# Attention in steps of four heads instead of two, its matmuls grouped by the way they divide TensorE's array

## The chip, the cores and the metric

The kernel runs on one core of a Trainium2 chip. The metric is the time of one execution on the device in microseconds (us). The engines have short names in the profile: PE is TensorE's matmuls, PEld its weight loads, DVE is VectorE, ACT is ScalarE, POOL is GpSimd, and SP issues most of the DMAs. Each engine works through its own instructions in the order in which the program lists them.

## What is computed

Attention over 2 batches of 8 heads with 768 positions and head dimension 64, then a mixture of 8 experts of which each token takes two, then an MLP, all in float32:

```python
scores = q @ k.T / 8 - slope[h] * dist          # kept: the first 8 keys, and the 96 last before the query
a = softmax(where(keep, scores, -1e9))
x = (a @ v) as [1536 tokens, 512]
logits = x @ w_gate + log1p(exp(x @ w_noise)) * noise     # top two experts, softmax over them
y = sum over the two experts of weight * (relu(x @ w1[e]) @ w2[e])
out = silu(y @ w_in) @ w_out
```

## The kernel before

The 1536 queries are 12 tiles of 128 (six of a batch). A tile's queries see at most 232 keys: the 96 before the tile, the 8 global ones and its own 128 (`WK`); the first tile of a batch (0 and 6) sees only its own 128 (`wd`). All of it is written in one order by hand (`tc.manual_schedule()`), so an engine takes its instructions in the order in which the loop at the end of the attention part calls the helpers.

That loop runs over steps `s`, four for a tile `n`, each with one pair of heads `c`. A step does, in this order: `scores(s)` (two matmuls that each use 64 rows of the array, one for each head of the pair, into the banks `h` and `y0` or `y1`; VectorE then adds the bias and takes the minimum, one head at a time, into `sb` and `mn`); `expo(s)` (ScalarE's exponential of each head into `pn`, with its sum); `p_t(s - 2)` (TensorE transposes the `pn` of two steps ago through the identity, ScalarE copies the result to `pts`); and `av(s - 3)` (the products with the values, each of which uses 64 columns of the array, into the bank `y3`; after a tile's last pair VectorE copies them to `xt`). A float32 matmul that is no transpose runs as two passes, which the trace lists one by one.

Between these the loop puts, by the step's place in its tile: the loads of q, k and v two tiles ahead; `prep_q` and `prep_k` for the next tile (four transposes each, copied by ScalarE and VectorE to `qh` and `kth`); `post` of the tile before, as a generator in parts (the gates' products `pg` with 64 columns each, the transposes of `xt`, VectorE's scaled copy `xn`, the gates' transpose, and VectorE's product `lp` and sum into `L`); the load and the split of the experts' first weights; and `route`, a generator in thirteen pieces, once for each group of tiles (0 to 3, 4 to 7, 8 and 9 inside the loop). Its pieces are small VectorE operations on logits; piece 8 is the maxima and the selection, piece 10 the matmuls that count with the selection (L620 to L623), piece 12 ends in the scatters of the tokens' rows by POOL. `routed(k)` takes the next k pieces; `R1` and `R2` say how many come before and after the step's transposes.

Transposed results go through three banks in turn (`tbank`: two of `tp` and `y2`): a transpose waits until the copy out of its bank, three uses earlier, is done.

After the loop come the experts and the MLP, which the change leaves as they are.

Of the kernel before, what the change touches and what calls it, by code (L numbers as in the profile page):

```python
# [20 lines left out]
P = 128  # L21
# [229 lines left out]
def attn_moe_mlp(ctx, tc, q, k, v, n_global, n_local, w_gate, w_noise, noise,  # L251
# [95 lines left out]
    # how many tokens chose an expert, and whether one chose more than two  # L347
# [10 lines left out]
    # three banks in turn  # L358
# [10 lines left out]
    # the values of a query tile's keys: the last PV of the tile before, the batch's first  # L369
    # NG (the global ones), those of its own tile, two neighbours in a partition  # L370
# [40 lines left out]
    # the tensor engine's clock rises only after it has been busy for a while  # L411
# [17 lines left out]
    # dist where a key is kept, far above any distance where not: a key of its own tile that comes  # L429
    # after the query counts as further off than any local one  # L430
# [23 lines left out]
    def late_consts():  # L454
# [9 lines left out]
        # summed over the partitions, this is the expert's first slot  # L464
# [36 lines left out]
    def scores(s):  # L501
# [4 lines left out]
        ps = [bank("h", 2), bank(f"y{s % 2}")]  # L506
        for j in range(2):
            r = slice(j * D, (j + 1) * D)
            nc.tensor.matmul(ps[j][:, :wd], QH[n][r, c, :], kt[r, c, o:o + wd], start=True, stop=True)  # L509
        SB[s] = awk.tile([P, 2, WK], F32, name="sb", bufs=3)  # L510
        MN[s] = awk.tile([P, 2], F32, name="mn", bufs=3)
        bt = bias1 if i else bias0
        for j in range(2):
            nc.vector.tensor_tensor_reduce(SB[s][:, j, :wd], ps[j][:, :wd], bt[:, 2 * c + j, :], 1.0, 3.0e38,  # L514
                                           op0=OP.add, op1=OP.min, accum_out=MN[s][:, j:j + 1])

    def expo(s):
        n, c = divmod(s, HP)
        wd = WK if tiles[n][1] else P
        if c == 0:  # L520
            SM[n] = xnp.tile([P, H], F32, name="sm", bufs=3)
        PN[s] = awk.tile([P, 2, WK], F32, name="pn", bufs=3)
        for j in range(2):
            nc.scalar.activation(PN[s][:, j, :wd], SB[s][:, j, :wd], AF.Exp, bias=MN[s][:, j:j + 1], scale=-1.0,  # L524
                                 accum_out=SM[n][:, 2 * c + j:2 * c + j + 1])

    def p_t(s):
        n, c = divmod(s, HP)
        nb, kr = (2, WK // 2) if tiles[n][1] else (1, P)
        p = tbank().rearrange("p (j a t) -> p j a t", j=2, a=2)  # L530
        for j in range(2):
            for a in range(nb):
                nc.tensor.transpose(p[:kr, j, a, :], PN[s][:, j, a:nb * kr:nb], ident)  # L533
        PT[s] = awk.tile([P, 2, 2, P], F32, name="pts")
        nc.scalar.copy(PT[s][:kr, :, :nb], p[:kr, :, :nb])

    def av(s):
        n, c = divmod(s, HP)
        i = tiles[n][1]
        if c == 0:  # L540
            OT[n] = bank("y3").rearrange("p (c t) -> p c t", c=HP)
        nb, kr = (2, WK // 2) if i else (1, P)
        for a in range(nb):
            for j in range(2):
                nc.tensor.matmul(OT[n][j * D:(j + 1) * D, c, :], VT[n][:kr, 2 * c + j, a, :], PT[s][:kr, j, a, :],  # L545
                                 start=(a == 0), stop=(a == nb - 1))
        if c == HP - 1:
            XT[n] = xnp.tile([P, HP, P], F32, name="xt", bufs=2)
            nc.vector.tensor_copy(XT[n], OT[n])

    # the gates' products of a token for each of the heads, whose sums are yet to be divided by
    def post(n, psum, direct=False):
# [3 lines left out]
        pg = psum()[:, :P]  # L556
        if direct:
            for c in range(HP):
# [3 lines left out]
        else:  # L562
            for u in range(2):
                for j in range(2):
                    nc.tensor.matmul(pg[j * D:(j + 1) * D], wgn[:, 2 * j + u, :], XT[n][:, 2 * j + u, :],
                                     start=(u == 0), stop=(u == 1))
# [3 lines left out]
        yield  # L570
# [6 lines left out]
        if direct:  # L577
            logits(pg)
        else:
            g = xnp.tile([P, P], F32, name="pg", bufs=2)  # L580
            nc.vector.tensor_copy(g, pg)
# [4 lines left out]
        if not direct:  # L586
            pl = psum()[:, :P]
            nc.tensor.transpose(pl, g, ident)
            yield
            logits(pl)  # L590

# [4 lines left out]
    # an expert's rows in blocks; of the first one's, the first two are read early  # L596
# [59 lines left out]
    # the slots of the other experts that no token took: all of them, if a token chose more than two  # L656
    # experts, as a slot in between is left out then
# [32 lines left out]
    routing, later = [], []  # L690
    R1, R2 = (0,1,1,1), (1,2,0,2)
    NS = NT * HP

    def start(g):
        if next(g, g) is not g:
            later.append(g)
# [10 lines left out]

    prep(0)
# [3 lines left out]
    for s in range(NS + 3):  # L712
        n, c = divmod(s, HP)
        if s < NS:
            scores(s)
            expo(s)
        if s == 0:
            prep(HP // 2)
# [6 lines left out]
        if c == 0:  # L725
            later = [g for g in later if next(g, g) is not g]
        routed(R2[c])
        if n < NT:
            if c == 0 and 2 <= n + 2 < NT:
                load_qk(n + 2)  # L730
                load_v(n + 2)
            if c == 1 and n + 1 < NT:
                start(prep_q(n + 1))
            if c == 2 and n + 1 < NT:
                start(prep_k(n + 1))
            if s == 1:
                late_consts()
            if s == 2:
                load_small()
            if s == 6:  # L740
                zero_fill()
        if c == 3 and n >= 1:
            start(post(n - 1, tbank))
        if c == 0 and n >= 2 and n - 2 in groups:
            routing.append(route(*groups[n - 2], tbank, True))
        if c == 1 and 2 <= n <= 10:
            load_half(n - 2)
        if c == 3 and 2 <= n <= 7:
            split_high(n - 2, True)
            split_low(n - 2, True)  # L750
    for g in later + routing:
        for _ in g:
            pass
    actx.close()

# [447 lines left out]
```

## Time and profile before

| | |
|---|---|
| time, median of 3 runs | 763.61 us (763.43 to 772.5) |
| span of the profiled execution | 765.0 us |
| TensorE busy | 744.1 us, 97% of the span |
| VectorE, ScalarE, GpSimd busy | 450.1, 270.8, 192.8 us |
| attention, to the first matmul of the experts | the first 137.55 us of the span |

The page gives the profiled execution by its span, from the first to the last instruction; the times of the runs are those of other executions. Busy time of TensorE is partly modelled, since matmuls are pipelined, so the starts of its instructions say more than their lengths. A bracket behind a row of a timeline says how long the engine was idle before it and what ended that.

### The profile page before, as it was taken

Reading aid. Unit: us, or ns where it says so; the run is one execution under the profiler, and the core shown is the slowest. Engines: PE = TensorE matmul, PEld = TensorE weight load, DVE = VectorE, ACT = ScalarE, POOL = GpSimd, SP = SyncE. Lnnn points to the kernel's source line nnn. Section 1 sums busy time; section 2 is a strip of 40 time slices with the busy share of each in tenths; the row PEclk is TensorE's granted clock in tenths of the full one; section 3 lists DMA queues with packets and bytes.
Section 4 is the critical chain, followed back from the end, with each engine's and each line's share of the span. In section 5 each row is a group of like instructions: output and inputs, shape, how many; then the busy total and the mean of one; then the engine's idle time right before and its main releaser. Section 6 shows DMA issues by size and latency. Waiting matters only on the chain.

```text
span 765.0 us, 11233 instructions
## 1 busy us (share of the span) xinstructions
PE 744.1 (97%) x4087; PEld 586.9 (77%) x4087; DVE 450.1 (59%) x986; ACT 270.8 (35%) x635; POOL 192.8 (25%) x178
## 2 busy tenths in 40 slices
PE   8998898999999999999999999999999999999996
PEld 4665565788777777777787777888888888888895
DVE  5567484647888898887888765574233332322332
ACT  6665573334333434434333345352122111111111
POOL 4135412334533234243434120422012000000000
PEclk9999896999999999999999999999999999999998
DMA  9868554267868587786868554652002010000100
GB/s 163 203 145 235 144 153 167 84 204 232 284 213 284 144 293 223 247 236 222 244 210 277 181 163 139 202 198 84 28 27 56 15 55 1 1 0 1 56 1 32
DMA packets 96278, 111.78 MB, mean 146 GB/s; under 512 B 36479, under 2 KB 65727, under 8 KB 96216
## 3 DMA queue, kind: packets, MB, share of 16 engines
q1 hardware_dynamic: 89096, 94.50, 41.7%
q0 software_dynamic: 6608, 16.10, 6.3%
q8 instruction: 34, 0.56, 0.3%
q10 hardware_dynamic: 512, 0.40, 0.2%
q14 instruction: 28, 0.23, 0.1%
HBM read 84.00 MB, written 32.51 MB: 152 GB/s over the span
## 4 chain that ended last, share of the span: by engine, by line
PE 87%; DVE 5%; issue 3%; ACT 2%; DMA 1%; another core or an unknown queue 1%; POOL 0%; SPq 0%; POOLq 0%; ACTq 0%; DVEq 0%
PE h L785 13%; PE h L788 12%; PE h L786 12%; PE y L820 11%; PE y L816 11%; PE y L821 11%; PE y L805 4%; PE y L545 3%; PE h L509 3%; PE tp L767 2%; PE tp L533 2%; ACT pn L524 1%; PE y L533 1%; PE tp L569 1%; PE tp L494 1%
## 5 line engine op out<-in xcount | busy, mean ns | idle before, releaser
L785 PE MATMUL h<-xh,u1h 128*128 128x448 f32 (+3 forms) x544 | 184.9, 352 | 0.0
L786 PE MATMUL h<-xh,u1l 128*128 128x448 f32 (+3 forms) x544 | 179.3, 341 | 0.0
L820 PE MATMUL y<-u2h,hh 128*128 128x512 f32 x368 | 145.3, 395 | 0.6 <-ACT hh L795 0.6
L821 PE MATMUL y<-u2l,hh 128*128 128x512 f32 x368 | 144.5, 393 | 0.0
L1112 DVE CAST hh<-h 128x256 fp32r<-128x256 f32 (+1 forms) x64 | 35.7, 558 | 149.8 <-ACT h L1111 149.7
L785 PEld LDWEIGHTS h<-xh,u1h 128*128 128x128 f32 x544 | 102.5, 188 | 26.0 <-issue 15.4
L788 PE MATMUL h<-xl,u1h 128*128 128x448 f32 (+3 forms) x544 | 120.0, 342 | 0.0
L786 PEld LDWEIGHTS h<-xh,u1l 128*128 128x128 f32 x544 | 102.7, 189 | 9.7
L816 PE MATMUL y<-u2h,hl 128*128 128x512 f32 x368 | 108.7, 394 | 0.7 <-DVE hl L796 0.7
L788 PEld LDWEIGHTS h<-xl,u1h 128*128 128x128 f32 x544 | 92.3, 189 | 9.0
L1111 ACT ACTIVATE h<-h 128x256 f32<-128x256 f32 (+1 forms) x64 | 30.4, 475 | 183.1 <-PE h L788 182.1
L887 POOL TENSOR_TENSOR co<-ct,co 128x512 f32<-128x512 f32 x32 | 41.4, 1292 | 175.5 <-issue 141.9
L816 PEld LDWEIGHTS y<-u2h,hl 128*128 128x128 f32 x368 | 68.9, 188 | 17.8 <-DVE hl L796 2.1
L820 PEld LDWEIGHTS y<-u2h,hh 128*128 128x128 f32 x368 | 69.2, 188 | 13.7 <-ACT hh L795 1.0
L821 PEld LDWEIGHTS y<-u2l,hh 128*128 128x128 f32 x368 | 69.2, 188 | 12.1
L1054 ACT ACTIVATE hw<-h 128x64 f32<-128x64 f32 x64 | 14.4, 224 | 130.6 <-DVE hl L796 125.2
L524 ACT ACTIVATE pn<-sb,mn 128x232 f32<-128x232 f32 (+1 forms) x96 | 44.8, 467 | 39.4 <-DVE mn L514 38.6
L770 DVE TENSOR_TENSOR xl<-tp,xh 128x512 fp32r<-128x512 f32 (+1 forms) x44 | 28.1, 643 | 45.6 <-ACT xh L769 45.5
L795 ACT ACTIVATE hh<-h 128x384 fp32r<-128x384 f32 (+2 forms) x72 | 31.3, 435 | 47.7 <-PE h L788 44.4
L796 DVE SCALAR_TENSOR_TENSOR hl<-h,hh 128x384 fp32r<-128x384 f32 (+2 forms) x72 | 34.4, 478 | 20.4 <-ACT hh L795 19.3
L324 POOL TENSOR_TENSOR u1l<-ra,u1h 128x1024 fp32r<-128x1024 f32 x16 | 41.9, 2617 | 5.6 <-ACT u1h L319 5.4
L514 DVE CUSTOM_DVE_ANT_0 sb<-h,bias 128x232 f32<-128x232 f32 (+1 forms) x48 | 18.2, 379 | 39.6 <-PE y L509 23.1
(219 smaller groups left out, 1053.8 us busy)
## 6 DMA issues: line engine op xcount, KB each, us to landing
ra<-in_moe_w SPq DMA_DIRECT2D x32, 512.0 KB
rb<-in_moe_w SPq DMA_DIRECT2D x32, 512.0 KB
cx<-in_moe_w_in SPq DMA_DIRECT2D x16, 512.0 KB
cx<-in_moe_w_out SPq DMA_DIRECT2D x16, 512.0 KB
xe<-XS SPq DMA_DIRECT2D x22, 256.0 KB
YS<-yx SPq DMA_DIRECT2D x18, 256.0 KB
WI<-co SPq DMA_DIRECT2D x16, 256.0 KB
WO<-co SPq DMA_DIRECT2D x16, 256.0 KB
```

What stands on the lines that cost most here:

```text
L324: (nc.gpsimd if pool else nc.vector).tensor_tensor(lo, raw[k], fr(hi), op=OP.subtract)
L524: nc.scalar.activation(PN[s][:, j, :wd], SB[s][:, j, :wd], AF.Exp, bias=MN[s][:, j:j + 1], scale=-1.0, accum_out=SM[n][:, 2 * c + j:2 * c ...
L785: nc.tensor.matmul(p, a, xh[:, c, s], start=(c == 0), stop=False)
L786: nc.tensor.matmul(p, b, xh[:, c, s], start=False, stop=False)
L788: nc.tensor.matmul(p, wh[:, c, o:o + P], xl[:, c, s], start=False, stop=(c == NC - 1))
L795: nc.scalar.activation(hh, p, AF.Relu)
L796: nc.vector.scalar_tensor_tensor(hl, p, 0.0, fr(hh), op0=OP.max, op1=OP.subtract)
L816: nc.tensor.matmul(PY[t][:s.stop - s.start], hl[:, s], uh[:, a, :], start=False, stop=(f == nf - 1))
L820: nc.tensor.matmul(PY[t][:s.stop - s.start], hh[:, s], uh[:, a, :], start=(f == 0), stop=False)
L821: nc.tensor.matmul(PY[t][:s.stop - s.start], hh[:, s], ul[:, a, :], start=False, stop=False)
L887: nc.gpsimd.tensor_tensor(o, a, o, op=OP.add)
L1112: nc.vector.tensor_copy(hh, p)
```

## The change

The loop now has two steps for a tile, each with four heads (`c2` is the half). `scores` computes two pairs into the same two banks, side by side, and `lowest` does VectorE's part of four heads; `expo` does four heads. `p_t` fills two banks, and `av` does two pairs. A step's order is now: `scores(s)`, VectorE's and ScalarE's work on them, `av(s - 2)`, in the first half of a tile the gates' products `pg`, then all that transposes: `prep_q` or `prep_k` of the next tile, `p_t(s - 1)`, the gates' transpose (first half) or `xt`'s (second half). `post` is cut accordingly: `xt`'s transposes and `xn` first, `pg` a step later, the gates' transpose after that. Two routing pieces run before `p_t` and three after it. Buffers for `sb` and `pn` are two of four heads each instead of three of two, `pts` four instead of two, `sm` four instead of three. The loads, the late constants and the zero fill are placed by the new steps; comments are dropped. The core of the diff:

```diff
+    def scores(s, cs=(0, 1), ps=None):
+        ps = ps or [bank("h", 2), bank(f"y{s % 2}")]
+        for c in cs:
+            for j in range(2):
+                r = slice(j * D, (j + 1) * D)
+                nc.tensor.matmul(ps[j][:, c * wd:(c + 1) * wd], QH[n][r, 2 * c2 + c, :], kt[r, 2 * c2 + c, o:o + wd],
+                                 start=True, stop=True)
+        return ps
...
     def p_t(s):
+        for c in range(2):
+            p = tbank().rearrange("p (j a t) -> p j a t", j=2, a=2)
...
+            PT[s, c] = awk.tile([P, 2, 2, P], F32, name="pts", bufs=4)
+            nc.scalar.copy(PT[s, c][:kr, :, :nb], p[:kr, :, :nb])
...
-    for s in range(NS + 3):
-        n, c = divmod(s, HP)
+    for s in range(NS + 2):
+        n, c2 = divmod(s, 2)
         if s < NS:
-            scores(s)
+            ps = scores(s, (0,) if s == 0 else (0, 1))
+            if s == 0:
+                prep(HP // 2)
+                scores(s, (1,), ps)
+            lowest(s, ps)
             expo(s)
-        later = [g for g in later if next(g, g) is not g]
-        routed(R1[c])
-        if 2 <= s < NS + 2:
-            p_t(s - 2)
-        if 3 <= s < NS + 3:
-            av(s - 3)
...
+        if s >= 2:
+            av(s - 2)
+        if c2 == 0 and n >= 2:
+            next(posts[n - 2])
         if n < NT:
+            if c2 == 0:
+                if n + 2 < NT:
+                    load_qk(n + 2)
+                if n + 1 < NT:
+                    run(prep_q(n + 1))
+            else:
+                if n + 2 < NT:
+                    load_v(n + 2)
+                if n + 1 < NT:
+                    run(prep_k(n + 1))
+                if 2 <= n <= 10:
+                    load_half(n - 2)
+                if 2 <= n <= 7:
+                    split_high(n - 2, True)
+                    split_low(n - 2, True)
...
+        if c2 and n >= 2 and n - 2 in groups:
+            routing.append(route(*groups[n - 2], tbank, True))
+        routed(2)
+        if 1 <= s <= NS:
+            p_t(s - 1)
+        if c2 == 0 and n >= 2:
+            run(posts.pop(n - 2))
+        routed(3)
+        if c2 and 1 <= n < NT:
+            posts[n - 1] = post(n - 1, tbank)
+            next(posts[n - 1])
```

## Rows read from the trace of the kernel before

**Rows 1.** Stretches (us): length, busy us of PE, PEld, DVE, ACT, POOL, granted clock, DMA.

```profile
30.20:39.96 9.76, 9.76 (x87) 6.76 (x86) 5.85 (x24) 6.70 (x23) 3.42 (x2) 1.00 0.68 157
69.49:83.84 14.35, 10.10 (x71) 6.49 (x70) 5.97 (x25) 7.08 (x26) 10.03 (x9) 0.89 0.85 266
104.85:114.68 9.83, 9.83 (x92) 6.86 (x91) 8.11 (x42) 6.81 (x22) 2.48 (x3) 1.00 0.46 149
114.68:137.55 22.87, 19.31 (x134) 13.47 (x134) 11.78 (x54) 8.57 (x26) 6.76 (x8) 0.70 0.41 143
```

**Rows 2.** Timeline of PE, 29.6 to 32.4: start, us, engine, line, out<-in, count.

```profile
29.61 0.33 PE L569 MATMUL tp<-ident,xt 128*128 128x128 f32 x1
29.78 0.49 PE L569 MATMUL tp<-ident,xt 128*128 128x128 f32 x3
...
30.00 0.27 PE L569 MATMUL tp<-ident,xt 128*128 128x128 f32 x1
30.20 0.46 PE L509 MATMUL h<-kth,qh 64*128 64x232 f32 x1
...
30.50 0.36 PE L509 MATMUL h<-kth,qh 64*128 64x232 f32 x1
...
30.79 0.37 PE L533 MATMUL tp<-ident,pn 128*116 128x128 f32 x1
31.00 0.49 PE L533 MATMUL tp<-ident,pn 128*116 128x128 f32 x3
...
31.42 0.33 PE L545 MATMUL y<-pts,vt 116*64 116x128 f32 x2
31.58 0.50 PE L545 MATMUL y<-pts,vt 116*64 116x128 f32 x6
...
32.08 0.30 PE L588 MATMUL y<-ident,pg 128*128 128x128 f32 x1
32.31 0.46 PE L509 MATMUL h<-kth,qh 64*128 64x232 f32 x1
```

**Rows 3.** Timeline of DVE and ACT in the same step.

```profile
31.00 0.40 DVE L514 CUSTOM_DVE_ANT_0 sb<-h,bias 128x232 f32<-128x232 f32 x1 [1.80 <-PE y L509]
31.33 0.39 DVE L514 CUSTOM_DVE_ANT_0 sb<-y,bias 128x232 f32<-128x232 f32 x1
31.44 0.49 ACT L524 ACTIVATE pn<-sb,mn 128x232 f32<-128x232 f32 x1 [1.20 <-DVE mn L514]
31.93 0.47 ACT L524 ACTIVATE pn<-sb,mn 128x232 f32<-128x232 f32 x1
```

**Rows 4.** Timeline of DVE, 46.4 to 47.7: the two copies of a tile.

```profile
46.40 0.69 DVE L549 COPY xt<-y 128x512 f32<-128x512 f32 x1 [0.40 <-PE y L545]
47.01 0.68 DVE L496 COPY kth<-tp 128x512 f32<-128x512 f32 x1
```

**Rows 5.** Groups by form, 20.44 to 59.6: busy us, mean ns, idle before.

```profile
L487 ACT ACTIVATE qh<-tp 128x512 f32<-128x512 f32 x4 | 2.4, 594 | 0.0
```

**Rows 6.** Timeline of DVE in tile 6: routing's selection, and the gates' product and sum.

```profile
61.52 0.36 DVE L614 MAX8 top<-lgs 128x8 f32<-128x8 f32 x4
61.92 0.19 DVE L615 TENSOR_TENSOR sels<-lgs,top 128x32 bf16<-128x32 f32 x1
...
62.80 0.29 DVE L573 TENSOR_TENSOR lp<-y,rs 128x128 f32<-128x128 f32 x1
63.12 0.38 DVE L575 TENSOR_REDUCE L<-lp 128x16 f32<-128x128 f32 x1
```

**Rows 7.** Timeline of all engines in tile 7, where attention pauses.

```profile
78.03 0.40 DVE L514 CUSTOM_DVE_ANT_0 sb<-h,bias 128x232 f32<-128x232 f32 x1 [4.29 <-remote]
...
78.53 0.70 PE L533 MATMUL y<-ident,pn 128*116 128x128 f32 x4 [2.17 <-issue]
...
80.27 0.56 ACT L535 COPY pts<-tp 116x512 f32<-116x512 f32 x1
...
80.88 1.12 PE L545 MATMUL y<-pts,vt 116*64 116x128 f32 x8 [1.65 <-ACT pts L535]
```

**Rows 8.** A stretch after that pause, columns as in rows 1.

```profile
81.00:87.00 6.00, 6.00 (x36) 4.12 (x36) 2.40 (x12) 3.08 (x11) 0.46 (x1) 0.50 0.99 237
```

More of the change, by code (lines that the diff above doesn't have):

```diff
@@ L517, in expo @@
     def expo(s):
-        n, c = divmod(s, HP)
+        n, c2 = divmod(s, 2)
         wd = WK if tiles[n][1] else P
[L520 to L525, printed above, removed]
+        if c2 == 0:
+            SM[n] = xnp.tile([P, H], F32, name="sm", bufs=4)
@@ L527, in p_t @@
+        PN[s] = awk.tile([P, 4, WK], F32, name="pn")
+        for g in range(4):
+            nc.scalar.activation(PN[s][:, g, :wd], SB[s][:, g, :wd], AF.Exp, bias=MN[s][:, g:g + 1], scale=-1.0,
+                                 accum_out=SM[n][:, 4 * c2 + g:4 * c2 + g + 1])
     def p_t(s):
-        n, c = divmod(s, HP)
+        n, c2 = divmod(s, 2)
         nb, kr = (2, WK // 2) if tiles[n][1] else (1, P)
[L530 to L533, printed above, removed]
@@ L534, in p_t @@
-        PT[s] = awk.tile([P, 2, 2, P], F32, name="pts")
-        nc.scalar.copy(PT[s][:kr, :, :nb], p[:kr, :, :nb])
+        for c in range(2):
+            p = tbank().rearrange("p (j a t) -> p j a t", j=2, a=2)
+            for j in range(2):
+                for a in range(nb):
+                    nc.tensor.transpose(p[:kr, j, a, :], PN[s][:, 2 * c + j, a:nb * kr:nb], ident)
+            PT[s, c] = awk.tile([P, 2, 2, P], F32, name="pts", bufs=4)
+            nc.scalar.copy(PT[s, c][:kr, :, :nb], p[:kr, :, :nb])
@@ L537, in av @@
     def av(s):
-        n, c = divmod(s, HP)
+        n, c2 = divmod(s, 2)
         i = tiles[n][1]
-        if c == 0:
+        if c2 == 0:
             OT[n] = bank("y3").rearrange("p (c t) -> p c t", c=HP)
         nb, kr = (2, WK // 2) if i else (1, P)
[L543 to L546, printed above, removed]
@@ L547, in av @@
-        if c == HP - 1:
+        for c in range(2 * c2, 2 * c2 + 2):
+            for a in range(nb):
+                for j in range(2):
+                    nc.tensor.matmul(OT[n][j * D:(j + 1) * D, c, :], VT[n][:kr, 2 * c + j, a, :],
+                                     PT[s, c - 2 * c2][:kr, j, a, :], start=(a == 0), stop=(a == nb - 1))
+        if c2:
             XT[n] = xnp.tile([P, HP, P], F32, name="xt", bufs=2)
@@ L561, in post @@
                                  start=True, stop=True)
[L562 to L566, printed above, removed]
         p = psum()
@@ L586, in post @@
         if not direct:
+            pg = psum()[:, :P]
+            for u in range(2):
+                for j in range(2):
+                    nc.tensor.matmul(pg[j * D:(j + 1) * D], wgn[:, 2 * j + u, :], XT[n][:, 2 * j + u, :],
+                                     start=(u == 0), stop=(u == 1))
+            g = xnp.tile([P, P], F32, name="pg", bufs=2)
+            nc.vector.tensor_copy(g, pg)
+            yield
             pl = psum()[:, :P]
             nc.tensor.transpose(pl, g, ident)
-            yield
             logits(pl)
@@ L688, in load_x @@
         reads.append(ld)
[L690 to L696, printed above, removed]
+    routing = []
+    NS = 2 * NT
     def routed(k):
@@ L706, in prep, with run @@
                 pass
+    def run(g):
+        for _ in g:
+            pass
     prep(0)
@@ L751, in attn_moe_mlp @@
-    for g in later + routing:
-        for _ in g:
-            pass
+        routed(2)
[7 more added lines that the diff above has]
+            next(posts[n - 1])
+    for g in routing:
+        run(g)
     actx.close()
```

59 lines of the change are left out of this document (19 added, 40 removed).

## The prediction

> **What bounds the kernel now.** I read first the table of stretches, cut at the start of attention's query tiles. In an undisturbed tile TensorE is busy for all of 9.76 us at full clock, VectorE for 5.85 and ScalarE for 6.70 [rows 1]; so attention is bound by TensorE, and what leaves TensorE there shortens the kernel, until another engine sets the pace. Tile 7 takes 14.35 us and the end of attention (its last tile, to the first matmul of the experts) runs at a mean clock of 0.70 [rows 1]. What comes after is not touched by the change.
>
> Then I read TensorE's timeline, start by start. Inside one kind of matmul the starts are 0.11 us apart (29.78 to 30.00, two steps), but from the last transpose to the first score matmul it takes 0.20, and from the first transpose of a group to the second 0.17 after column-split matmuls and 0.21 after row-split ones [rows 2]. I call F the transposes (the whole array), R the scores (64 rows each) and C the products with the values (64 columns each). A float32 matmul other than a transpose runs as two passes, and the passes of a pair of heads run side by side. So a change of kind costs about 0.09 at the border and, in the second start, 0.05 (C), 0.06 to 0.10 (F), 0.10 (R: 0.30 between the passes, where 232 columns at the pace of 128 in 0.11 are 0.20) [rows 2].
>
> **The change, part by part.**
>
> *Fewer changes of kind.* Before, each of the four steps of a tile goes R, F, C, F: 0.19 + 0.19 + 0.14 + 0.15 = 0.67, and 2.7 in a tile. After, each of two steps goes R, C, F: 0.19 + 0.14 + 0.15 = 0.48, and 0.96 in a tile. Saved: 1.7 us, so TensorE alone would need 9.76 - 1.7 = 8.0 us. The entry to C straight after R isn't in the trace; I take that after F. Its bounds are the entries seen, 0.14 to 0.19, which is nothing beside the rest.
>
> Four passes in a row on one row half are not in the trace either: only the first two are, 0.30 apart. The ends are 0.20 (the next weights load under the running passes, as in the transposes) and 0.30 (they don't); I take 0.20, as in F loads do hide. The Trainium skill ("TensorE: Matmul & The Clock Gate", Part 3, The mechanism) says that a weight load overlaps running matmuls only where the row groups differ. By that rule a step's four passes would be 0.30 apart; in this trace the transposes, on the same rows, come 0.11 apart all the same, which speaks against it, but no row shows it for R.
>
> *Hand-offs inside a step.* With TensorE at 8.0 us, the question is whether the others deliver in time. Each new step is a chain, as its last matmuls need a bank that is freed by work that hangs on its first ones. The three banks of the transposes go round in order, and counting uses (gates, q, two of p, gates' transpose; k, two of p, x) the gates' transpose gets the bank of q, and x's transposes that of k.
>
> Step A (first half of a tile): scores' last pass at 0.30 + 0.20 + 0.20 = 0.70; VectorE starts 0.50 after a last pass and ScalarE's exponentials 0.44 after VectorE's start (30.50, 31.00, 31.44) [rows 2, 3]: 1.20 and 1.64. Four exponentials at a pitch of 0.49 [rows 3] end at 3.60. Only then, in ScalarE's order, comes the copy of q, 0.59 [rows 5]: 4.19. TensorE goes on 0.05 after a ScalarE copy ends (80.27 + 0.56, 80.88) [rows 7], transposes the gates and reaches the next scores 0.23 later (32.08 to 32.31) [rows 2]: 4.47 us.
>
> Step B: VectorE's four at a pitch of 0.33 [rows 3] run from 1.20 to 2.52; then the copy of x, 0.61, and of k, 0.68 [rows 4] until 3.81. The transposes of x start at 3.86, take 0.17 + 0.22, and the border 0.20: 4.45 us.
>
> Together 8.92 us against 9.76: a gain of 0.84 a tile, half of the 1.7. The other half turns into waits in front of the gates' and x's transposes. This assumes that VectorE waits for all four passes of a bank. The ends are 0.30 + 0.50 = 0.80 (it waits for the first head's alone) and 1.20; I take 1.20, since every reduction of the trace starts after its bank's last pass. The Trainium skill ("PSUM — Partial Sum Buffer", PSUM bank collisions raise a hardware error) says to guard the memory by bank, not by address, which would give the same 1.20; no row can show it. With 0.80 the gain would be up to 1.6 a tile.
>
> Eight tiles (2 to 5, 8 to 11) gain 0.84, that is 6.7; tiles 6 and 7, which are narrower or half narrow, I put at 0.5 each (an estimate between 0 and 0.84). Tiles 0 and 1 and the last steps I put at nothing: the first steps now wait for both halves of q and k before any reduction, and at the end as many waits as before stand in line. The loads keep their order and their distance of two tiles; that of the values is issued half a tile later, but before too it stood waiting on SP. Sum: -7.7.
>
> *Routing's pieces.* Before, they are dealt out singly between the steps, and a tile with them takes 9.83 [rows 1]: free. Now five run per step, two before the transposes of p and three after. In the step that starts a group (a B), eight small VectorE operations and the two for the sums stand before the scaling of x: at 0.2 each (the selection's row has 0.19) [rows 6] 2.0, so that from 3.81 with the scaling (0.61, as the copy of its shape [rows 4]) it ends at 6.4, or 2.0 into the next A; with ScalarE's two pieces in between I say 2.2. A's reductions start there instead of at 1.20: 1.0 late. Then, in that A, the eighth and tenth piece (the selection, and the matmul that reads it) come in one go behind the gates' transpose. TensorE waits: 0.50 until VectorE has the transpose, 0.62 for its product and sum (62.80 to 63.12, and as much again), 0.40 for the maxima (61.52 to 61.92), 0.19 for the selection [rows 6], 0.05: 1.76, then some 0.15 for the matmuls and 0.20 for the border, where 0.23 stood. That is 1.9 more; with 1.0, 2.9 in each of the two groups whose pieces fall among full steps (the third falls at the end): +5.8. The bounds are 0 (VectorE ahead) and twice that.
>
> Tile 7's pause (VectorE idle for 4.29 us, with the scatters on POOL) [rows 7] has no cause in the trace that the change removes; I leave it, with its 4.6 us over an ordinary tile, as an uncertainty.
>
> **Sum.** -7.7 + 5.8 = -1.9 us. The profiled execution spans 765.0 us, 1.4 over the median of 763.6; I take the difference to the median: **761.7 us**.
>
> **Rivals.**
> *TensorE stays the bound.* Hand-offs hide, routing is free: 8 x 1.76 + 2 x 1.0 = 16.1, so 747.5. For it: ScalarE's 6.70 and VectorE's 5.85 are below 8.0. Against it: sums don't matter where each step is one chain.
> *The clock falls (slower than before).* In tile 7 TensorE was idle for 2.17 and 1.65 us within 5 us [rows 7], and then ran six us at 0.50, 1.2 GHz in place of 2.4 [rows 8], 3.0 lost. Routing's A would have idle times of some 1.4 and 1.8. If both groups drop the clock: 761.7 + 6.0 = 767.7. It decides from the point where the idle times reach those of the rows.
> *The passes of R stay 0.30 apart.* Last pass at 0.90, both chains 0.2 longer, a gain of 0.44: 8 x 0.44 + 0.5 = 4.0, and 763.6 - 4.0 + 5.8 = 765.4. The skill's rule above gives this.
> *The change doesn't do what it says:* the 0.09 and 0.05 to 0.10 are waits of another sort, which stay; then only routing's cost is left, 769.4. Against it: the border is the same 0.20 wherever kinds meet.
>
> **Chances.** Forecast 0.43 (its own range 756 to 767, with the bounds of the bank's wait and of routing), TensorE the bound 0.12, clock 0.20, R's passes 0.15, no effect 0.10. A range of 750 to 771 leaves out the first rival and the far end of the clock's and the last one's, about 0.2. Over 2% (about what a measurement of this kernel can tell from no change) would be below 748.3 or above 778.9: faster 0.10, same 0.85, slower 0.05.
>
> **What would show it.** Starts within R 0.20 apart, three changes of kind a step; a tile at 8.9 us with TensorE waiting for ScalarE's copy of q and VectorE's copy of k; a wait of the prefix matmul for the selection in tiles 6 and 10. I am wrong if a tile takes 8.0 or less, if routing's steps are no longer than others, or if the end of attention moves by itself.

## The result, and the profile after

The changed kernel takes 768.97 us (median of 20 runs, 764.67 to 771.71) where the kernel before takes 764.45 (median of 20): a ratio of 1.0055 with an interval of 1.0042 to 1.0069, so about 4.5 us lost. The forecast was a small gain, 761.7 against 763.6. The number lies in the range of 750 to 771, the sign is wrong, and nearest to what came is the rival in which the clock falls (767.7).

The profiled executions span 767.2 and 765.0 us, 2.2 apart; experts start at 139.51 instead of 137.55. In every run the time is 1.7 to 1.9 above the span of the same execution. So the profiled execution of the changed kernel (768.96) stands at its median, and that of the kernel before, at some 766.8 by that difference (an estimate), about 2.3 above its own. So what can be followed in these traces is a loss of 1.97 over attention's 131 us (the first score matmul comes 0.01 earlier). From the starts of the score matmuls in the two timelines of TensorE:

| tile | before, us | after, us | difference |
|---|---|---|---|
| 0, 1 | 4.93, 8.84 | 5.03, 7.49 | +0.10, -1.35 |
| 2, 3, 5, 9 | 9.76, 9.76, 9.91, 9.76 | 8.82, 8.84, 8.83, 8.83 | -3.87 |
| 4 | 9.74 | 10.10 | +0.36 |
| 6 | 9.88 | 14.51 | +4.63 |
| 7, 8 (one of them has the pause) | 14.35, 11.25 | 9.01, 14.60 | -1.99 |
| 10 | 9.83 | 14.44 | +4.61 |
| 11 to the experts | 22.87 | 22.35 | -0.52 |

The gains sum to 7.73, the losses to 9.70. First the undisturbed tile. The table of stretches of the changed kernel, columns as in [rows 1]: tile 3's two steps, and tile 4's first:

```profile
28.00:32.43 4.43, 4.24 (x46) 3.46 (x45) 2.35 (x10) 3.10 (x11) 0.00 (x0) 1.00 1.04 226
32.43:36.84 4.41, 4.13 (x42) 3.30 (x41) 3.87 (x13) 3.41 (x13) 1.92 (x2) 1.00 0.90 189
36.84:42.53 5.69, 4.49 (x46) 3.52 (x45) 3.89 (x12) 3.08 (x11) 3.28 (x3) 1.00 0.95 229
```

The timeline of TensorE through tile 3 (L512 the scores, L545 p's transposes, L603 the gates' transpose, L577 the transposes of x):

```profile
28.00 0.46 PE L512 MATMUL h<-kth,qh 64*128 64x232 f32 x1
...
28.30 0.36 PE L512 MATMUL h<-kth,qh 64*128 64x232 f32 x1
...
28.50 0.36 PE L512 MATMUL h<-kth,qh 64*128 64x232 f32 x1
...
28.70 0.36 PE L512 MATMUL h<-kth,qh 64*128 64x232 f32 x1
...
...
32.17 0.33 PE L603 MATMUL tp<-ident,pg 128*128 128x128 f32 x1 [0.19 <-ACT qh L487]
32.43 0.46 PE L512 MATMUL h<-kth,qh 64*128 64x232 f32 x1
...
36.25 0.66 PE L577 MATMUL y<-ident,xt 128*128 128x128 f32 x4 [0.28 <-DVE kth L496]
36.84 0.46 PE L512 MATMUL h<-kth,qh 64*128 64x232 f32 x1
```

And the engines that it waits for, from the timelines of VectorE and ScalarE in the same tile, with GpSimd's at the end:

```profile
29.20 0.40 DVE L525 CUSTOM_DVE_ANT_0 sb<-h,bias 128x232 f32<-128x232 f32 x1 [0.39 <-PE y L512]
29.64 0.49 ACT L535 ACTIVATE pn<-sb,mn 128x232 f32<-128x232 f32 x1 [1.33 <-DVE mn L525]
31.55 0.57 ACT L487 ACTIVATE qh<-tp 128x512 f32<-128x512 f32 x1
35.51 0.68 DVE L496 COPY kth<-y 128x512 f32<-128x512 f32 x1
35.98 2.36 POOL L324 TENSOR_TENSOR u1l<-ra,u1h 128x1024 fp32r<-128x1024 f32 x1
36.11 2.25 DVE L567 TENSOR_SCALAR rs<-sm 128x8 f32<-128x8 f32 x1
```

Four passes of the scores start at 0, 0.30, 0.50 and 0.70. TensorE waits at two places in the tile, for ScalarE's copy of q and for VectorE's copy of k. Last two lines: beside GpSimd's subtraction, which ends at 38.34, an instruction on eight columns takes 2.25 us, to 38.36, where the same one takes 0.17 in tile 10. Behind it come xn and then the reductions of tile 4's scores (39.31, 2.47 into the step instead of 1.20), and that step takes 5.69. Now the tiles with routing, 6 and 10, both steps of each:

```profile
55.77:64.75 8.98, 4.74 (x51) 3.60 (x50) 8.28 (x32) 4.04 (x13) 3.44 (x2) 0.85 0.63 148
64.75:70.28 5.53, 5.23 (x40) 4.27 (x37) 3.25 (x17) 2.41 (x11) 0.00 (x0) 0.63 0.15 41
102.72:110.24 7.52, 4.82 (x52) 3.74 (x51) 5.90 (x31) 4.12 (x13) 0.00 (x0) 0.97 0.57 174
110.24:117.16 6.92, 6.92 (x44) 5.76 (x41) 4.28 (x21) 2.86 (x10) 0.39 (x1) 0.54 0.01 2
```

In the first step of each, TensorE is busy for 4.8 of 7.5 and 9.0 us. In the second, TensorE is busy nearly throughout, at a granted clock of 0.63 and 0.54 (mostly 1.2 GHz instead of 2.4). TensorE's waits in the two first steps, from its timeline (L634 is the matmul that reads the selection):

```profile
61.25 0.33 PE L603 MATMUL tp<-ident,pg 128*128 128x128 f32 x1 [0.63 <-ACT qh L487]
64.50 0.21 PE L634 MATMUL y<-sels,tri 128*128 128x32 bf16 x1 [2.92 <-DVE sels L629]
...
107.03 0.70 PE L545 MATMUL tp<-ident,pn 128*116 128x128 f32 x4 [0.77 <-DVE pg L600]
108.38 0.33 PE L603 MATMUL y<-ident,pg 128*128 128x128 f32 x1 [0.65 <-ACT qh L487]
110.00 0.21 PE L634 MATMUL tp<-sels,tri 128*128 128x32 bf16 x1 [1.29 <-DVE sels L629]
```

Tile 6's wait is longer than tile 10's by 1.63. The timelines of GpSimd and of VectorE there:

```profile
59.55 1.05 POOL L317 TENSOR_SCALAR u2h<-rb 128x1024 fp32r<-128x1024 f32 x1 [5.84 <-DMA rb<-in_moe_w]
60.68 2.39 POOL L324 TENSOR_TENSOR u2l<-rb,u2h 128x1024 fp32r<-128x1024 f32 x1
```

```profile
59.79 0.85 DVE L58 SCALAR_TENSOR_TENSOR td<-td,ta 128x32 f32<-128x32 f32 x1
60.67 0.19 DVE L60 SCALAR_TENSOR_TENSOR td<-L,td 128x32 f32<-128x32 f32 x1
60.90 2.22 DVE L61 TENSOR_TENSOR lgs<-td,nz 128x32 f32<-128x32 f32 x1
```

Two small instructions of the routing take 0.85 and 2.22 instead of the 0.18 and 0.19 of tile 10; each ends within 0.05 of the end of the GpSimd instruction that ran when it started (60.60 and 63.07). Not every small instruction is held like that. The gates' sum in tile 5 keeps its length beside the subtraction that runs from 51.35 to 53.72:

```profile
51.80 0.37 DVE L585 TENSOR_REDUCE L<-lp 128x16 f32<-128x128 f32 x1
```

Last, the pause that [rows 7] shows in tile 7 stands in tile 8 now. VectorE's timeline:

```profile
85.10 0.29 DVE L600 COPY pg<-tp 128x128 f32<-128x128 f32 x1 [3.25 <-remote]
...
89.45 0.29 DVE L583 TENSOR_TENSOR lp<-y,rs 128x128 f32<-128x128 f32 x1 [4.06 <-remote]
```

As before, it ends with no releaser inside the core. Its first part ends while the first group's scatters run on GpSimd (77.91 to 88.14), its second 1.31 after the last of them.

### The profile page after: what moved, and what is told of

Read it like the earlier page. It is cut to its first block, busy times and chain, and to the rows that moved or that the text cites. A ratio compares the mean times of both kernels' runs of the same rounds, so it can differ in the third digit from the quotient of the medians.

```text
span 767.2 us, 11187 instructions
## 1 busy us (share of the span) xinstructions
PE 732.5 (95%) x4087; PEld 590.0 (77%) x4087; DVE 453.1 (59%) x986; ACT 269.1 (35%) x635; POOL 192.8 (25%) x178
## 4 chain that ended last, share of the span: by engine, by line
PE 78%; DVE 10%; ACT 4%; issue 4%; DMA 1%; SPq 1%; another core or an unknown queue 1%; POOL 0%; DVEq 0%; POOLq 0%; ACTq 0%
PE h L805 12%; PE h L808 11%; PE h L806 11%; PE y L840 10%; PE y L836 10%; PE y L841 10%; PE y L825 3%; PE h L512 2%; PE tp L787 2%; ACT pn L535 2%; DVE sb L525 2%; PE y L558 1%; DVE ct L901 1%; DMA rc<-WO 1%; DMA qt<-in_q 1%
## 5 line engine op out<-in xcount | busy, mean ns | idle before, releaser
L319 ACT CAST u1h<-ra 128x1024 fp32r<-128x1024 f32 x37 | 38.8, 1050 | 5.6 <-DMA ra<-WI 4.3
```

The source lines that it names most:

```text
L319: nc.scalar.copy(hi, raw[k])
```

## The experiments

My theory after the result had four parts. The length of an undisturbed step is the chain of hand-offs and not TensorE's work. The three routing pieces behind p's transposes make TensorE wait for the selection. That wait takes the clock down in the step behind. And GpSimd's long instructions hold back small ones of VectorE. The rivals were that changes of kind still set the step, that the loss sits in the pauses of tile 8 and of the end, and that the clock fell for another reason. The runs stand in three sets with their own runs of the kernel before; the second set ran on another chip, where all is some 12 us shorter, so only ratios are compared between sets.

**Set 1** (before: 764.69).

*e1: two and two pieces of routing a step instead of two and three.*

```diff
-        routed(3)
+        routed(2)
```

> The changed kernel with two routing pieces behind a step's transposes instead of three, so that the selection (piece 8) and the matmul that reads it (piece 10) fall into different steps. Theory (TensorE's wait for the selection, and the clock that falls with it, cost 4.6 us in each of tiles 6 and 10 and turn the gain into a loss): no prefix matmul waits for the selection, the clock stays at 1.00 in tiles 6 and 10, these tiles take 9 to 11 us instead of 14.5, and the time falls by 5 to 9 us against the changed kernel, to 0.993 to 0.998 of the kernel before. Rival (VectorE's extra work in these steps costs the time, wherever the pieces stand): tiles 6 and 10 stay above 13 us, and the time stays at 1.005 of the kernel before.

764.37 us, ratio 0.9998 (0.9978 to 1.0018). The stretches of tile 6 and of tile 10:

```profile
55.99:61.27 5.28, 4.31 (x46) 3.39 (x45) 4.64 (x21) 3.40 (x13) 1.45 (x2) 1.00 1.04 251
61.27:67.33 6.06, 3.72 (x43) 2.74 (x42) 5.67 (x26) 2.96 (x13) 1.99 (x1) 0.99 0.44 116
101.28:106.74 5.46, 4.51 (x46) 3.53 (x46) 4.02 (x20) 3.48 (x12) 0.00 (x0) 1.00 0.78 240
106.74:112.33 5.59, 4.38 (x46) 3.54 (x46) 5.17 (x28) 3.38 (x12) 0.00 (x0) 1.00 0.02 3
```

11.34 and 11.05 us instead of 14.51 and 14.44, all at full clock; the wait for the selection is gone in tile 10 and 0.85 in tile 6. Taking one piece out of each step brings back the loss, and no more: TensorE now waits 1.49 and 1.21 for the copy of k, behind VectorE's pieces. The direction is the theory's, the size falls short of it: 4.6 us under the changed kernel where 5 to 9 were expected, and tiles of just over 11 us where 9 to 11 were.

*e2: work for TensorE in the wait.* Eight matmuls whose result the next one overwrites stand ahead of the matmul that reads the selection, in the first two groups.

```diff
-        pos = psum()[:, :m * E].rearrange("p (t e) -> p t e", e=E)
+        pb = psum()
+        if t1 < 10:
+            for _ in range(8):
+                nc.tensor.matmul(pb, idle[:, :P], idle, start=True, stop=True)
+        pos = pb[:, :m * E].rearrange("p (t e) -> p t e", e=E)
```

> The changed kernel with eight matmuls on zeros (128x512, bfloat16) in front of the matmul that waits for the selection, in the two groups inside the loop: TensorE computes while it would wait, nothing else is changed. Theory (of the 4.6 us of tiles 6 and 10, about 2.5 are the clock at half rate, 6.9 us for the step after the wait in tile 10 where others take 4.4): the clock stays at 1.00 through tile 10, its second step takes 4.4 to 4.8 us, and the time falls by 2 to 5 us against the changed kernel, to 0.999 to 1.003 of the kernel before. Rival (the clock does not fall because of this wait): no change, or slower by the matmuls that overrun the wait, up to 1 us.

767.02 us, ratio 1.0029 (1.0003 to 1.0056). The stretches of tiles 6 and 10:

```profile
55.05:63.16 8.11, 6.59 (x60) 4.36 (x59) 7.20 (x32) 4.04 (x13) 3.49 (x2) 1.00 0.70 164
63.16:66.90 3.74, 3.35 (x39) 2.65 (x36) 3.20 (x17) 2.29 (x11) 0.00 (x0) 1.00 0.18 53
101.02:110.31 9.29, 7.74 (x60) 4.83 (x59) 5.89 (x31) 4.12 (x13) 0.00 (x0) 0.86 0.46 143
110.31:114.95 4.64, 4.47 (x42) 3.60 (x40) 3.51 (x17) 2.76 (x10) 0.00 (x0) 0.92 0.00 0
```

With work that is of no use, the second steps take 3.74 and 4.64 instead of 5.53 and 6.92, at a clock of 1.00 and 0.92. So 1.8 and 2.3 us of these steps were the clock's. In tile 10 the filler outlasted the wait (9.29 instead of 7.52, where at most 1 us was expected) and ate most of it. Tile 6's first step is shorter than the changed kernel's 8.98 in spite of the filler, as GpSimd's instructions met others of VectorE there: lgs took 0.91 instead of 2.22, the selection 0.99. The time of this run alone can't be told from that of the changed kernel, as the intervals overlap; the stretches can.

*e3: q's copy on VectorE, from tile 1 on.*

```diff
-        nc.scalar.activation(QH[n][:, c0:c1], p, AF.Copy, scale=-1.0 / math.sqrt(D))
+        if n:
+            nc.vector.tensor_scalar(QH[n][:, c0:c1], p, -1.0 / math.sqrt(D), None, op0=OP.mult)
+        else:
+            nc.scalar.activation(QH[n][:, c0:c1], p, AF.Copy, scale=-1.0 / math.sqrt(D))
```

> The changed kernel with the copy of q (scaled, 128x512) on VectorE instead of ScalarE, for all tiles but the first, so that the gates' transpose no longer waits for ScalarE's four exponentials. Theory (each step is a chain; in the first half of a tile the chain is scores, minimum, exponentials, copy of q, gates' transpose, 4.43 us where TensorE's own work is 3.95): the first half takes 3.9 to 4.1 us in undisturbed tiles, the second stays at 4.41, and the time falls by 2 to 4 us against the changed kernel. Rival (TensorE's own work is already the bound, or VectorE gets into its own way): 4.4 as before, or longer, and no gain.

766.96 us, ratio 1.0036 (1.0017 to 1.0055). First steps take 4.15 (27.89 to 32.04) instead of 4.43, second steps stay at 4.40 (32.04 to 36.44). TensorE's work is the same; only the engine that copies q, and with it the end of the chain, was changed. The 4.15 are just over the expected 3.9 to 4.1: the gates' transpose waits for nothing any more, and what is left is TensorE's own work. The waits for the selection stay, 3.99 in tile 6 and 1.56 in tile 10. At 0.28 in each of the nine tiles from 2 to 10 the shorter steps would be worth 2.5 us (an estimate); the ratios to before give 1.5, which the intervals don't resolve.

*e5: two more changes of kind in each step.* A matmul with half the array's columns, on zeros, stands ahead of each step's transposes of p and is overwritten by them.

```diff
-            p = tbank().rearrange("p (j a t) -> p j a t", j=2, a=2)
+            pb = tbank()
+            if c == 0:
+                nc.tensor.matmul(pb[:D, :D], idle[:, :D], idle[:, :D], start=True, stop=True)
+            p = pb.rearrange("p (j a t) -> p j a t", j=2, a=2)
```

> The changed kernel with one small column-split matmul (zeros, 64 columns) in front of each step's transposes of p, which puts two more changes of kind into each of 24 steps; it costs TensorE 0.3 to 0.4 us a step by the starts of the kernel before. Theory (hand-offs set a step's length, with 0.5 us of slack on TensorE): a tile stays at 8.8 to 9.0 us and the time within 2 us of the changed kernel. Rival (changes of kind still set the length): 0.7 us more a tile, 6 to 9 us in all, 1.014 to 1.017 of the kernel before.

770.19 us, ratio 1.0062 (1.0037 to 1.0087), as the changed kernel's 1.0055. TensorE's timeline in a first step:

```profile
33.09 0.22 PE L544 MATMUL y<-idle 128*64 128x64 bf16 x1
...
34.23 0.33 PE L606 MATMUL tp<-ident,pg 128*128 128x128 f32 x1
34.48 0.46 PE L512 MATMUL h<-kth,qh 64*128 64x232 f32 x1
```

The step still takes 4.42 (30.06 to 34.48) and the one behind it 4.41: the wait at L606 is gone, filled by the extra matmul and its two changes of kind. With e3's 4.15, TensorE has some 0.28 to spare in a first step; changes of kind within that cost nothing here, and so the last of the saved ones bring nothing.

**Set 2** (before: 751.96). In none of its four traces does VectorE or TensorE pause in tiles 7 and 8 as in tile 8 of the changed kernel, whatever the kernel.

*e6: e1 and e3 together.*

```diff
-        nc.scalar.activation(QH[n][:, c0:c1], p, AF.Copy, scale=-1.0 / math.sqrt(D))
+        if n:
+            nc.vector.tensor_scalar(QH[n][:, c0:c1], p, -1.0 / math.sqrt(D), None, op0=OP.mult)
...
-        routed(3)
+        routed(2)
```

> Both edits at once: two and two pieces of the routing a step (alone it gave 764.4 us, 0.9998 of before) and the q copy on VectorE from tile 1 on (alone A steps of 4.15 us instead of 4.43). Theory (the hand-offs' length sets each undisturbed step, the routing's places set the rest, and the two add): A steps 4.1 to 4.2 us, B steps 4.4, tiles 6 and 10 about 10.6 to 11.3 us, a granted clock of 0.95 or more in tiles 6 and 10; time 761.5 to 763.5 us, ratio 0.996 to 0.9985 of before. Rival (the q copy on VectorE lengthens the routing's pieces there, so that the second gain is eaten): ratio 0.999 to 1.001, with waits for VectorE's k copy over 1.5 us in tiles 6 and 10.

749.43 us, ratio 0.9953 (0.9934 to 0.9973): better than expected and less than before. First steps 4.14, second 4.41. Tile 10 takes 10.33. Tile 6 takes 12.54 with a wait of 2.15 for the selection, and the clock is 0.81 there and 0.65 in the step behind; GpSimd's subtraction from 60.79 to 63.19 lies beside the small instructions of VectorE, of which one takes 1.74. So that expectation (0.95 or more) held in tile 10 only.

*e4: q's copy on VectorE, and four and two pieces, all ahead of p's transposes.*

```diff
-        routed(2)
+        routed(2 if c2 else 4)
...
-        routed(3)
```

> The q copy on VectorE from tile 1 on, and the routing's pieces dealt four in each A step and two in each B step, all ahead of p's transposes, none behind the exps' hand-off. Theory (a piece on VectorE ahead of the k copy lengthens a B step, a piece in an A step has room behind the exps): B steps with routing about 5.0 us, A steps with routing about 5.0, tiles 6 and 10 about 10 to 10.8 us at a granted clock of 0.95 or more; time 760 to 763 us, ratio 0.994 to 0.998. Rival (four pieces in front of p's transposes bring back a wait of TensorE for the selection, as three and two did): one A step of 6.5 us or more in tiles 6 or 10 with TensorE at the prefix matmul's line waiting for the selection, and a granted clock under 0.8 behind it; ratio 1.000 to 1.005.

755.53 us, ratio 1.0032 (1.0017 to 1.0047): slower than e6 by 6.1, and the expectation failed. Tile 10 is short, 8.99 us and no wait for the selection. Tile 6 is not: 11.47 us, with waits of 1.62 and 2.01 for VectorE in its second step, at a clock of 0.81, and 0.67 in the step behind. Most of the loss is at the end, where only six pieces a tile (eight in e6) leave the third group late. The stretch from the last step to the experts in this kernel:

```profile
107.75:123.97 16.22, 12.12 (x110) 9.88 (x109) 11.51 (x53) 6.35 (x19) 9.81 (x10) 0.82 0.64 227
```

and in e6:

```profile
108.82:120.59 11.77, 10.16 (x110) 8.20 (x109) 9.23 (x43) 6.26 (x19) 5.97 (x7) 1.00 0.79 262
```

In e4, TensorE waits there 1.98 for the third group's selection (0.54 in e6), and the clock is 0.82 instead of 1.00. Tile 10's wait and fallen clock have moved to the end. Of the 5.0 us between the two profiled executions, 3.4 stand before the experts' start; the others come behind it and are not followed here.

*e7: GpSimd's split of the weights with one input.* The subtraction of the high half is left out of six weight pieces by that, and nothing else.

```diff
-        (nc.gpsimd if pool else nc.vector).tensor_tensor(lo, raw[k], fr(hi), op=OP.subtract)
+        if pool == "one":
+            nc.gpsimd.tensor_scalar(lo, raw[k], 1.0, 1.0, op0=OP.mult, op1=OP.mult)
+        else:
+            (nc.gpsimd if pool else nc.vector).tensor_tensor(lo, raw[k], fr(hi), op=OP.subtract)
```

> GpSimd's subtraction of two inputs that makes the weights' low halves during the attention (six times, 2.36 us each) becomes a product with constants of the same tile and one input; the low halves of those weights are wrong by that, nothing else is left out. Theory (GpSimd's instruction with two inputs keeps VectorE's small instructions from going, 0.16 us becoming 2.25 us, and TensorE's hand-offs no longer cover it): no small VectorE instruction over 1 us in the tiles 3 to 7, tile 4's A step 4.4 to 4.6 us instead of 5.69, tile 6's A step 1 to 2 us shorter than 8.98; time 765.5 to 767.8 us, ratio 1.001 to 1.004. Rival (the long VectorE instructions come from something else that lies there by chance, or any GpSimd instruction does it): one of 1.2 us or more stays in these tiles, tile 4's A step 5.5 to 5.8 us, ratio 1.0045 to 1.0065.

752.84 us, ratio 1.0016 (0.9988 to 1.0043). The profiled execution took 758.12, one of the three longest of ten, so only its stretches are read. GpSimd and VectorE in tile 6, from their timelines:

```profile
58.17 1.05 POOL L317 TENSOR_SCALAR u2h<-rb 128x1024 fp32r<-128x1024 f32 x1 [7.36 <-DMA rb<-in_moe_w]
59.18 1.04 POOL L325 TENSOR_SCALAR u2l<-rb 128x1024 fp32r<-128x1024 f32 x1
```

```profile
58.49 0.76 DVE L58 SCALAR_TENSOR_TENSOR td<-td,ta 128x32 f32<-128x32 f32 x1
59.29 0.98 DVE L60 SCALAR_TENSOR_TENSOR td<-L,td 128x32 f32<-128x32 f32 x1
```

The first steps of tile 6 take 7.63 here and 8.94 in e8, which keeps the subtraction; the waits for the selection are 1.60 and 2.91. So the subtraction costs 1.3 us there. But my account of it was wrong: an instruction of one input holds VectorE back just as well (0.98, to 60.27, where GpSimd ends at 60.22), only not as long. Tile 4 tells nothing: its first step takes 4.42 here and 4.42 in e8 too, where the subtraction, still in place, started 0.20 us later than in the changed kernel (36.18 instead of 35.98), behind the eight-column instruction's start at 36.17.

*e8: the first group's scatters ahead of a split of weights that waits for its load.*

```diff
-                if 2 <= n <= 7:
+                if 2 <= n <= 7 and n != 6:
...
+        if s == 13:
+            split_high(4, True)
+            split_low(4, True)
```

> In step 13 GpSimd's split of the weights, which waits for its load until 74.2 us, comes after the routing's pieces of that step, so that the first group's eight scatters no longer stand behind it. Theory (the pauses of VectorE and TensorE of 2.6 to 4.1 us, which end with no releaser inside the core, go with the scatters): the scatters run from about 68 to 78 us, the pauses stand in tile 7, and tile 8's two steps take 4.4 to 5 us instead of 8.29 and 6.31; time 766 to 770 us, ratio 1.002 to 1.007. Rival (the pauses belong to the place in the program and not to the scatters): they stay in tile 8, whose steps take 7 us or more in sum above two undisturbed ones' 8.83 by at least 4 us.

754.34 us, ratio 1.0032 (1.0014 to 1.005). The scatters run from 69.08 to 79.28, and there is no pause in tile 7 nor in tile 8, so that this run decides nothing about what makes the pauses: on this chip there were none to move. But a loss of 0.3% is there without them, so the loss does not need the pause of tile 8. The run shows something else, too. The stretches of tile 10, e8 and then e7:

```profile
95.43:102.92 7.49, 4.80 (x52) 3.72 (x51) 5.90 (x31) 4.12 (x13) 0.00 (x0) 1.00 0.57 175
102.92:107.21 4.29, 4.12 (x43) 3.30 (x40) 3.52 (x17) 2.76 (x10) 0.00 (x0) 1.00 0.01 4
```

```profile
93.94:101.46 7.52, 4.81 (x51) 3.74 (x51) 5.90 (x31) 4.12 (x13) 0.00 (x0) 0.96 0.57 174
101.46:108.30 6.84, 6.84 (x43) 5.68 (x41) 4.23 (x20) 2.86 (x10) 0.30 (x1) 0.54 0.01 2
```

Behind a first step of the same length and with the same waits, the second one takes 4.29 at a clock of 1.00 in the one and 6.84 at 0.54 in the other. The fall is worth 2.55 us, and after such waits it comes in some executions and not in others.

**Set 3** (before: 765.87).

*a1: the changed kernel again.* No edit.

> The changed kernel once more, beside the other two of this set. Theory (its loss stands in tiles 6 and 10: a wait for the selection, and a granted clock that falls to about 0.55 in the step behind it, in most executions but not in all): ratio 1.003 to 1.006 of before on whatever times this set has, tile 10's A step 7.4 to 7.6 us, its B step 6.9 us where the granted clock is under 0.6 and 4.3 to 4.5 us where it stays at 1.00, no pause of VectorE and TensorE over 2.5 us in tile 8 if before is near 752 us, such pauses if it is near 764 us. Rival (the loss belongs to the pauses in tiles 8 and 11 of the first set, and not to tiles 6 and 10): ratio 0.996 to 1.000 where the pauses are gone.

769.02 us, ratio 1.0049 (1.0021 to 1.0076), with pauses of up to 4.99 us in tile 8, as the theory had it for a set with these times. Tile 6 took 14.21 us, with the same wait and clock (2.81, and 0.65 in the second step); in tile 10 the clock held, with a second step of 4.29 behind a first one of 7.49. Tile 4 took 8.82: GpSimd's subtraction started at 36.20, 0.02 after the eight-column instruction had ended. Six traces have the pieces three and two and nothing to fill the wait (the changed kernel, a1, e3, e5, e7, e8). Behind tile 6's wait for the selection, of 1.60 to 3.99, the next step ran at a granted clock of 0.50 to 0.67 in all six. Behind tile 10's, of 1.29 to 1.56, it ran at 0.54, 0.72 and 0.54 in three (the changed kernel, e3, e7) and at 1.00 in the other three.

*e6 again.*

> Two and two pieces of the routing a step and the q copy on VectorE once more, beside the changed kernel in one set. Theory (its A steps are 0.28 us shorter in the nine tiles from 2 to 10, and tiles 6 and 10 lose less): ratio 0.994 to 0.9975 of before, 5 to 8 us under the changed kernel in this set. Rival (the first figure came from executions in which the clock happened to hold): ratio 0.999 to 1.002.

762.28 us, ratio 0.9962 (0.9942 to 0.9983), 6.7 under the changed kernel. Its experts start at 132.09, in set 2 at 120.59: 11.5 us apart, as the spans are (759.4 and 747.9). What the chips differ by lies in attention, in tile 8, tile 11 and the end.

*e9: e6, and GpSimd's splits of two weight pieces behind the first group's scatters.*

```diff
-                if 2 <= n <= 7:
+                if n in (2, 3, 4, 7):
                     split_high(n - 2, True)
...
+        if s == 13:
+            for u in 3, 4:
+                split_high(u, True)
+                split_low(u, True)
```

> As the kernel with two and two pieces and the q copy on VectorE, and GpSimd's splits of the fourth and fifth weight halves (a product of 1.04 us and a subtraction of two inputs of 2.4 us each) come behind the first group's scatters in step 13, so that none lies beside the first group's small VectorE instructions. Theory (GpSimd's subtraction stretched two of them to 1.24 and 1.74 us and through them the selection, for which TensorE waited 2.15 us): no VectorE instruction of 128x32 elements over 0.4 us in tile 6, the wait for the selection under 0.7 us, tile 6's B step 5 to 6 us instead of 7.98; 1.5 to 3.5 us under the kernel without this edit, ratio 0.991 to 0.994. Rival (the loads behind the splits come later and cost at the experts' start what tile 6 gains): first matmul of the experts not earlier, ratio 0.9945 to 0.999.

759.6 us, ratio 0.9917 (0.9887 to 0.9947): the shortest, 6.3 under before and 9.4 under the changed kernel. It is 2.7 under e6; all its seven executions (up to 760.76) are below all twelve of e6 (from 761.16). The two stretches of tile 6:

```profile
55.36:59.91 4.55, 4.21 (x46) 3.39 (x46) 4.17 (x21) 2.68 (x11) 0.00 (x0) 1.00 1.07 269
59.91:64.84 4.93, 3.52 (x42) 2.79 (x42) 4.62 (x28) 3.19 (x13) 0.00 (x0) 1.00 0.42 103
```

Tile 6 takes 9.48 instead of 12.44 in e6 of this set, at full clock and without a wait for the selection. The pause has moved into tile 7 (64.84 to 78.11), from VectorE's timeline:

```profile
76.31 0.69 DVE L499 COPY kth<-tp 128x512 f32<-128x512 f32 x1 [2.85 <-remote]
```

The first group's scatters run from 65.48 to 75.71 here and from 69.74 to 79.94 in e6, whose pause of 3.16 ended at 78.37 in tile 8. On this chip the pauses go along with the scatters; in set 2 the scatters run and there is no pause. Scatters alone are therefore not the cause, and what else it takes stays open.

## Why the prediction was wrong, and what of it was right

The step that failed is the routing term, +5.8. It priced TensorE's waits for the selection as if the clock stayed at 1.00 behind them, and VectorE's pieces at 0.2 us each. The runs show in its place a clock that falls behind the wait, at 1.8 us in tile 6 and 2.6 in tile 10, and pieces of up to 2.22 us beside GpSimd's split, which cost tile 6 another 1.3.

*Fewer changes of kind: right.* The four passes come 0.30, 0.20 and 0.20 apart, as taken. The Trainium skill ("TensorE: Matmul & The Clock Gate", Part 3, The mechanism) has a sentence by which loads overlap running matmuls only between row groups, which would have kept 0.30; the trace of after contradicts that for score matmuls on the same rows (28.30, 28.50, 28.70). TensorE's own work came out somewhat longer than the 8.0 priced: 4.15 in e3's first step and 4.13 in the second (4.41 less the wait of 0.28), so that 1.5 of the 1.7 were saved. The rival of the passes falls, and so do the ones in which TensorE stays the bound or the change has no effect.

*Hand-offs: right, part by part.* Predicted for the first step: VectorE at 1.20, ScalarE at 1.64, q's copy done at 4.19, the step 4.47. Measured: 1.20, 1.64, 4.12, 4.43. For the second: k's copy done at 3.81, the step 4.45; measured 3.76 and 4.41. Together 8.92 and 8.84. VectorE starts 0.50 after the fourth pass and not after the second, with which the first head is done; the bank rule of the Trainium skill ("PSUM — Partial Sum Buffer", PSUM bank collisions raise a hardware error) would give that. e3 and e5 show that this chain, and nothing of TensorE's, sets the first step, if only by 0.28. That the gains in the table sum to 7.73 beside the predicted 7.7 is chance: tile 1, put at nothing, gave 1.35, tile 4 gave nothing, and what tiles 6 and 10 gained is inside their losses.

*Routing: the wait right, its consequences not in the sum.* Tile 10's first step is 3.1 longer than an undisturbed one; 2.9 was predicted, from waits that are there. The sum is nearer than its parts: the gates' transpose starts 1.49 late, where 1.0 was taken (108.38, 5.66 into the step, against 4.17 in tile 3), and the selection adds 1.60 instead of 1.9, with a wait of 1.29 instead of 1.76. Two things were left out of the forecast.

The first is the clock. It was a rival with a chance of 0.20 and a price of 3.0 in each group. It fell behind the wait in both groups of the profiled execution, and the price is 2.6 in tile 10 (6.92 against a1's 4.29) and 1.8 in tile 6 (5.53 against e2's 3.74). Forecast and rival shared the same waits of 1.4 and 1.8, and the condition I wrote, "from the point where the idle times reach those of the rows" (2.17 and 1.65), was too strict: in tile 10 waits of 0.77, 0.65 and 1.29 sufficed in one execution and not in another. The forecast should have been a mixture with the clock's fall at least as likely as not: in the six traces it came behind tile 6's wait each time, behind tile 10's three times. That the rival's 767.7 lies near the result is in part luck, as its price was too high and GpSimd's share was not in it.

The second is in the term for tile 6: the pieces were priced at 0.2 each, and two of them took 0.85 and 2.22 beside GpSimd's split, for a wait of 2.92 instead of 1.76. e7, with a shorter instruction in place of the subtraction, puts this at 1.3, e9 takes it away. The same holding back cost tile 4's first step 1.26 in the profiled execution and nothing in a1. Before, too, small VectorE instructions met that split. In tile 6 of the kernel before, beside GpSimd's subtraction from 64.13 to 66.49:

```profile
64.42 2.12 DVE L632 TENSOR_TENSOR slh<-un,s 128x32 f32<-128x32 f32 x1
68.09 0.44 PE L545 MATMUL y<-pts,vt 128*64 128x128 f32 x4 [1.17 <-ACT pts L535]
```

The same instruction takes 0.18 in tile 10 of the changed kernel. It stood behind the selection then, and TensorE, with work queued until 66.9, waited 1.17 for what came behind it on VectorE and ScalarE. The change used up such cover. The rows were in the trace of before, and I did not ask which pieces were held there, and what hid it.

*Sum.* Forecast -1.9, profiled +2.0: tile 10 is 2.55 over its predicted 11.89 (9.83 - 0.84 + 2.9) and tile 6 2.23 over its 12.28 (9.88 - 0.5 + 2.9), tile 4 1.2 over, and tile 1 1.35 under; the other rows together are 0.7 under. In tile 6 the clock's 1.8 and the held pieces' 1.3 are more than the 2.23, so the rest of it came 0.9 shorter than priced. The 2.3 by which the medians' 4.5 goes beyond the 2.2 of the two profiled executions lie in the kernel before, whose profiled execution was that much above its median; what made it so is not followed here.

*Pauses:* left as an uncertainty, rightly. The pause moved from tile 7 to tile 8, at the same cost for the two together.

## What to carry to other kernels

When a change takes work from the bounding engine, the next bound can be the longest chain of hand-offs within a step; here it could be added up from the rows of before within 0.1 us (8.92 against 8.84). But the cover goes with the work: list every wait and every slowed instruction that was hidden under the bounding engine, and price each as exposed, the clock behind it too. Work dealt out in pieces has to be dealt anew when the steps get longer: the same pieces in other places took away a loss of 0.5% (e1); with q's copy on VectorE (e6) and GpSimd's splits elsewhere (e9) too, the change gained 0.8%.

## What the hardware showed that I had not expected

Some of VectorE's small instructions end 0.02 to 0.05 us after the GpSimd instruction that ran when they started: 0.17 became 2.25, 0.19 became 2.22, 0.98 beside one of 1.04. In these traces it happened to those with two inputs in SBUF and to the TENSOR_SCALAR form with one. Others whose inputs lie in SBUF kept their length beside such a subtraction: the gates' sum (0.37 in tile 5), a reciprocal (0.20 in a1, at 36.22) and the maxima (0.36 in e2, at 61.51). So did those that read PSUM (the scores' reductions, 0.40 in tile 5). The Trainium skill ("SBUF — State Buffer", SBUF: two separate sides) says that VectorE in its fast modes, or with two inputs from SBUF, and GpSimd share a pair of ports as a lock that is held for the whole instruction; the trace agrees for those with two inputs, down to 32 columns and fewer (0.17 became 1.37 on 8 columns in e1, at 71.45). In which mode the TENSOR_SCALARs ran no run shows.

After the same idle times the granted clock of the next step was 0.54 in two executions and 1.00 in two others (after and e7; e8 and a1).

The same kernel (e6) reached its experts 11.5 us earlier on one chip than on another. Of that, 5.0 are tile 8, where VectorE pauses beside the scatters on the one and not on the other; most of the rest is in tile 11 and the end. The cause is open.
